# Reordering the first weight loads of a fused top-k attention and cosine feed-forward kernel

## The chip, the cores and the metric

The kernel runs on one core of a Trainium2 chip. The metric is device time in microseconds (us) of one execution. Four executions of the kernel before took 1467.93 to 1472.03 us, median 1469.47 us. In the text and in the profile, PE is TensorE (matmul), ACT is ScalarE, DVE is VectorE, POOL is GpSimd and SP is SyncE, which here only issues transfers (DMAs). "ACTq" and "SPq" are the queues from which those engines issue transfers.

## The reference

```python
def _attn_ref(q, k, v):                       # 8 batches, 8 heads, 576 positions, 64 wide
    scores = scale * np.matmul(q, k.transpose(0, 1, 3, 2))
    kth = np.partition(scores, -32, axis=-1)[..., -32:-31]
    scores = np.where(scores >= kth, scores, -1000000000.0)
    scores = scores - np.max(scores, axis=-1, keepdims=True)
    attn = np.exp(scores)
    attn = attn / (np.sum(attn, axis=-1, keepdims=True) + 1e-09)
    return np.matmul(attn, v).astype(np.float32)

def _moe_ref(x, w_in, w_out):                 # 4608 tokens, 512 -> 2048 -> 512
    h = x @ w_in
    g = h * np.cos(h)
    return (g @ w_out).astype(np.float32)
```

The attention output, with its heads laid side by side, is the x of the feed-forward block. The two weight matrices come as float64, all other inputs as float32.

## The kernel before, in words

A **unit** is 128 tokens by one pair of heads; there are 144 of them. One **slot** of the main loop (`slot`, line 720) handles each unit through a software pipeline. In slot i, DVE searches the 32 largest scores of unit i, with rows of 576 folded to 288 (`topk_first`, three `topk_round`s, and after the middle of the slot `topk_round(u, 3)` for the lesser halves, which reads `low`). POOL makes `low` for it (`fold_sum` L274, `fold_low` L283). ACT masks and exponentiates unit i-1 (L390, L392, L400) and takes the scores of unit i+1 out of PSUM (`take_scores`, L241 and L244). POOL splits the words of unit i-2 (`split`, L433 and L435), and SP writes them to DRAM and reads them back transposed (L443, L449). On even slots PE multiplies the transposed weights of two units by v (`values`, L486), and DVE writes the result to xT (L495). A slot starts on DVE with the fold L256.

Feed-forward work is fed into the slots as PE finds room (`feed`, `ff1` L546, `ff2` L621). Which piece goes where is fixed when the program is built, by a credit and by counts of what is ready; one of these counts is how many weight chunks were decoded by the slot before. An `ff2` piece also needs `g`, which POOL multiplies at L608.

**Weights.** They are float64 in DRAM and are decoded on the chip. There are 32 chunks of 128 rows by 512 numbers (512 KB each), 16 of w_in and 16 of w_out. `load_weights` (line 105) loads chunks into staging tiles `st`; the queue is ACT's unless another is given. `decode_first` does two ACT operations for each chunk (L136, L139), `decode_second` one DVE shift (L147), and `decode_third` one POOL addition (L157). In each slot the shifts stand in DVE's program after the third round of the search, so a shift that waits holds the rest of the search. The additions stand in POOL's program after `fold_low` of that slot and ahead of the `split` of the next. `decode_first` stands in ACT's program at the end of a slot.

**Order of loads before.** The prologue (from line 812) loads q and k of the first two pairs of heads and 2 chunks on SP's queue, then 6 chunks on ACT's queue, and then decodes 4 chunks. Slot 0 and slot 1 load q and k of pairs 2 and 3 and then v, on SP's queue; slot 1 loads 4 chunks, slots 2 and 3 load 3 chunks each, later slots 2 each, all on ACT's queue. The built program gives every transfer one of eight semaphores, and a transfer is issued only once the earlier transfer with the same semaphore has landed.

`BUSY` is a set of slots in which DVE makes `low` itself, with one more fold (L264), instead of POOL.

Of the kernel before, what the change touches and what calls it, by code (L numbers as in the profile page):

```python
# [30 lines left out]
def kernel(  # L31
# [9 lines left out]
    nc = tc.nc  # L41
# [6 lines left out]
    NP = H // 2  # L48
# [37 lines left out]
    for i in range(DF // CW):  # L86
        w = consts.tile([P, NC, CW], F32, tag=f"w_in{i}", name=f"w_in{i}")
# [4 lines left out]
    for f in range(NF):  # L92
        w = consts.tile([P, DM], F32, tag=f"w_out{f}", name=f"w_out{f}")
        w_out.append(w)
        chunks.append((moe_w_out[f * P : (f + 1) * P, :], w))
    CHUNKS, XB = 7, 4
    BUSY = range(7, 11)
    ff = {"live": 0, "tick": 0, "now": 0, "credit": 0.0, "end": False, "kind": 0, "half": 0, "open": 0}

    wq = {"next": 0, "loaded": deque(), "second": deque(), "third": deque(), "done": 0, "ready": 0}  # L100

    def staged(spare=0):
        return sum(c[2] == spare for k in ("loaded", "second", "third") for c in wq[k])

    def load_weights(n, queue=None):
        queue = queue or nc.scalar
        for _ in range(n):
            i = wq["next"]
            if i >= len(chunks):
                return  # L110
            src, dst = chunks[i]
            if not DECODE:
                queue.dma_start(out=dst, in_=src)
                wq["next"] = wq["done"] = i + 1
                continue
            spare = i < 3 * XB and i % 2 == 1 and staged(1) < XB
            if spare:
                st = ffw.tile([P, CW, 2], I32, tag="x", name="st", bufs=XB)
            elif staged() + ff["live"] >= CHUNKS:
                return  # L120
            else:
                st = ffw.tile([P, CW, 2], I32, tag="g", name="st", bufs=CHUNKS)
            queue.dma_start(out=st.rearrange("p w i -> p (w i)"), in_=src)
            wq["loaded"].append((st, dst, int(spare)))
            wq["next"] = i + 1
# [4 lines left out]
    def decode_first(n):  # L130


        for _ in range(min(n, len(wq["loaded"]))):
            st, w, spare = wq["loaded"].popleft()
            lo, hi = st[:, :, 0], st[:, :, 1]
            nc.scalar.activation(  # L136
                out=w, in_=hi.bitcast(F32), func=AF.Prelu, scale=2.0**-111, alpha=2.0**32
            )
            nc.scalar.mul(out=lo, in_=lo.bitcast(U32), mul=2.0**-29)  # L139
            wq["second"].append((st, w, spare))  # L140

    def decode_second(n):

        for _ in range(min(n, len(wq["second"]))):
            st, w, spare = wq["second"].popleft()
            wi = w.bitcast(I32)
            nc.vector.tensor_scalar(  # L147
                out=wi, in0=wi, scalar1=3, scalar2=None, op0=ALU.logical_shift_left
            )
            wq["third"].append((st, w, spare))  # L150

    def decode_third():

        while wq["third"]:
            st, w, _ = wq["third"].popleft()
            wi = w.bitcast(I32)
            nc.gpsimd.tensor_tensor(out=wi, in0=wi, in1=st[:, :, 0], op=ALU.add)  # L157
            wq["done"] += 1
# [91 lines left out]
    def fold_high(u):  # L250

        s, sc = u["s"], u["sc"]
        if u["n"] not in BUSY:
            del u["sc"]
# [5 lines left out]
    def fold_now(u):  # L260

        s, sc = u["s"], u.pop("sc")
        u["low"] = work.tile([P, 2, HS], F32, tag="low", name="low", bufs=1)
        nc.vector.tensor_tensor(  # L264
            out=u["low"], in0=sc[:, :, 0:HS], in1=s[:, :, HS:S], op=ALU.min
        )

    def fold_sum(u):

        if not u["folds"]:  # L270
            return
        s = u["s"].bitcast(I32)
        u["low"] = work.tile([P, 2, HS], F32, tag="low", name="low", bufs=1)
        nc.gpsimd.tensor_tensor(  # L274
            out=u["low"].bitcast(I32), in0=s[:, :, 0:HS], in1=s[:, :, HS:S], op=ALU.add
        )

    def fold_low(u):

        if not u["folds"] or u["n"] in BUSY:  # L280
            return
        low = u["low"].bitcast(I32)
        nc.gpsimd.tensor_tensor(  # L283
            out=low, in0=low, in1=u["rest"][:, :, HS:S].bitcast(I32), op=ALU.subtract
        )
# [15 lines left out]
    def topk_first(u, w):  # L301

        u["top"] = tops[u["n"] % len(tops)]
        merges = w and w["folds"]
        if merges:
            merge_first(w)
        if u["folds"]:
            if u["n"] not in BUSY:
                fold_sum(u)
            fold_high(u)  # L310
        else:
            u["rest"] = work.tile([P, 2, S], F32, tag="rest", name="rest", bufs=1)
        if merges:
            merge_second(w)
        if u["folds"] and u["n"] in BUSY:
            fold_now(u)
        topk_round(u, 0, [lambda: bounds(w), lambda: distances(w)] if w else ())

    def topk_round(u, rnd, between=(), ahead=None):
        top, rest, lasts = u["top"], u["rest"], TOPK // 8 - 1  # L320
        end = TOPK - 1 - 8 * rnd
        at = top[:, :, end : end - 8 if rnd < lasts else None : -1, 0]
        if u["folds"]:
            search(
                at, rest[:, :, HS:S] if rnd == 0 else rest[:, :, 0:HS], rest[:, :, 0:HS], rnd < lasts,
                between if rnd < lasts else (),
            )
        else:
            search(at, u["s"] if rnd == 0 else rest, rest, rnd < lasts, between)
        if rnd < lasts:  # L330
            return
        del u["rest"]
        if u["folds"]:
            low = u.pop("low")
            for k in range(TOPK // 16):
                more = k < TOPK // 16 - 1
                if ahead and not more:
                    take_values(ahead)
                search(
                    top[:, :, 1 + 8 * k : 9 + 8 * k, 1], low, low, more,  # L340
                    () if more or rnd < lasts else between,
                )
# [10 lines left out]
    def merge_second(u):  # L353
        nc.vector.tensor_reduce(
            out=u["top"][:, :, TOPK - 1, 1], in_=u.pop("lesser"), axis=mybir.AxisListType.X,
            op=ALU.max,
        )
# [57 lines left out]
    def both(u):  # L415
        return [lambda: sums(u), lambda: reciprocal(u)] if u else ()
# [151 lines left out]
    def take_banks():  # L568
        while full:
            take, *what = full.popleft()  # L570
            take(*what)
# [117 lines left out]
    at_slot, at_once = {}, {}  # L689
# [7 lines left out]
    for n in range(NP, len(order)):  # L697
        i = last[order[n - 5]] if n >= 5 else 0
        load_at(max(i, 2 * NP + 2), load_qk, *order[n])
        i = last_values[order[n - 6]] if n >= 6 else 0  # L700
# [2 lines left out]
    for hp in range(NP):  # L703
        at_once[hp] = [(load_v, 0, hp)]
    for hp in range(2, NP):
        at_once[hp - 2].insert(0, (load_qk, 0, hp))


    for i, u in enumerate(units):
# [4 lines left out]
    def send(x):  # L714

        split(x)
        write_halves(x)
        transposes(x)

    def slot(i, u, w, x, z):  # L720
        n = 0 if i == 0 else 4 if i == 1 else 3 if i < NP else 2
        if i < NP:
            for load, b, hp in at_once[i]:
                load(b, hp)
        load_weights(n)
        if x:
            send(x)
        topk_first(u, w)
        fold_low(u)
        topk_round(u, 1)  # L730
        topk_round(u, 2)
        decode_second(NP)
        decode_third()
        made = scored.get(i, [])
        if z:
            take_banks()
        feed(1)

        for m in made:
            scores(m)  # L740
        if z:
            values(z)


        late = len(made) > 0

        decoding = i < 3 * NP
        if i % 2 or decoding:
            sines(1)
        if w:  # L750
            mask(w)
        take_banks()
        if w and late:
            exponentials(w)
        take_scores(units[i + 1])
        if w and not late:
            exponentials(w)
        topk_round(u, 3, both(w), z)
        if i in at_slot:
            load, b, hp = at_slot[i]  # L760
            load(b, hp)
        gate(1)
        feed(1 if len(made) == 2 else 2)
        take_banks()
        decode_first(NP)
        reduce_first()
        reduce_second()
        feed(1 if len(made) == 2 else 3)
        if i == LAST:
            sines(1)  # L770
# [43 lines left out]
        nc.tensor.matmul(tt[:, 0:P], ones, ones, start=True, stop=True)  # L814
    load_qk(0, 0)
    load_qk(0, 1)
    load_weights(2, nc.sync)
    scores(units[0])
    take_scores(units[0])
    load_weights(2 * NP - 2)  # L820
    decode_first(NP)
    for i in range(NU + 1):
        ff["end"] = i >= NU
        ff["credit"] = min(ff["credit"] + 5.0 - 0.9 * len(scored.get(i, [])), 5.3)
# [2 lines left out]
        u, w = (units[i - n] if 0 <= i - n < NU else None for n in range(2))  # L827
# [53 lines left out]
```

## Time and profile before

| | |
|---|---|
| Median of four executions | 1469.47 us |
| Profiled execution, its own time | 1468.81 us |
| Its span in the profile | 1467.0 us |
| Mean granted TensorE clock | 0.971 |
| PE busy / DVE busy / ACT busy / POOL busy | 95% / 93% / 74% / 79% of the span |

Busy shares are means over stages that differ. The slots start on DVE (first instruction at L256) at these times in us from the start of the span: slot 0 at 7.82, 1 at 28.98, 2 at 39.31, 3 at 52.94, 4 at 62.93, 5 at 73.33, 6 at 82.99, 7 at 93.04, 8 at 103.33, 9 at 114.44. A timeline line reads: start, time from the first start to the last end of the merged instructions, engine, line, operation, output <- inputs, shapes, count, and in brackets how long the engine stood idle before and what released it.

### The profile page before, as it was taken

Reading aid. Unit: us, or ns where it says so; the run is one execution under the profiler, and the core shown is the slowest. Engines: PE = TensorE matmul, PEld = TensorE weight load, DVE = VectorE, ACT = ScalarE, POOL = GpSimd, SP = SyncE. Lnnn points to the kernel's source line nnn. Section 1 sums busy time; section 2 is a strip of 40 time slices with the busy share of each in tenths; the row PEclk is TensorE's granted clock in tenths of the full one; section 3 lists DMA queues with packets and bytes.
Section 4 is the critical chain, followed back from the end, with each engine's and each line's share of the span. In section 5 each row is a group of like instructions: output and inputs, shape, how many; then the busy total and the mean of one; then the engine's idle time right before and its main releaser. Section 6 shows DMA issues by size and latency. Waiting matters only on the chain.

```text
span 1467.0 us, 30264 instructions
## 1 busy us (share of the span) xinstructions
PE 1387.3 (95%) x10290; PEld 995.7 (68%) x10290; DVE 1363.2 (93%) x5213; ACT 1087.1 (74%) x1911; POOL 1163.4 (79%) x814
## 2 busy tenths in 40 slices
PE   4278899999999999999999999999999999999998
PEld 2155667777777767777777777777777776777765
DVE  5999999999999999999999999999999999999831
ACT  4677777777777777777777777777777787777651
POOL 3977888888888887888888888888888888888510
PEclk6579999999999999999999999999999999999999
DMA  8787576656665576656765666656665456655300
GB/s 264 221 238 209 164 200 158 160 156 183 189 162 149 148 200 170 163 151 177 197 170 148 146 176 190 176 143 175 192 169 159 144 166 175 168 151 143 71 8 15
DMA packets 427433, 239.99 MB, mean 164 GB/s; under 512 B 375952, under 2 KB 392592, under 8 KB 427280
## 3 DMA queue, kind: packets, MB, share of 16 engines
q1 hardware_dynamic: 417552, 212.69, 54.7%
q10 hardware_dynamic: 9728, 25.38, 5.1%
q8 instruction: 81, 1.33, 0.4%
q14 instruction: 72, 0.59, 0.1%
HBM read 45.09 MB, written 101.19 MB: 100 GB/s over the span
## 4 chain that ended last, share of the span: by engine, by line
PE 84%; DVE 10%; ACT 4%; DMA 1%; issue 0%; POOL 0%; SPq 0%; ACTq 0%; POOLq 0%
PE o L621 32%; PE mm L546 31%; PE rim L486 10%; PE sc L229 8%; DVE top L361 4%; DVE rest L366 2%; PE rim L229 2%; DMA st<-in_moe_w_in_dram 1%; DVE rest L256 1%; ACT s L400 1%; ACT s L392 1%; DVE low L366 1%; DVE w_in L147 1%; ACT L400 0%; ACT x L562 0%
## 5 line engine op out<-in xcount | busy, mean ns | idle before, releaser
L546 PEld LDWEIGHTS mm<-xT,w_in 128*128 128x128 f32 x4608 | 536.6, 192 | 71.9 <-issue 64.1
L621 PE MATMUL o<-w_out,g 128*128 128x512 f32 x1152 | 541.5, 604 | 8.9 <-POOL g L608 7.6
L546 PE MATMUL mm<-xT,w_in 128*128 128x128 f32 x4608 | 539.9, 275 | 5.2 <-DVE xT L495 3.2
L361 DVE MAX8 top<-rest 128x8 f32<-128x288 f32 x1148 | 480.9, 454 | 0.0
L433 POOL COPY halves<-s 128x2304 uint16<-128x2304 uint16 x140 | 294.7, 2105 | 149.7 <-ACT s L400 148.8
L366 DVE MATCH_REPLACE8 rest<-top,rest 128x288 f32<-128x288 f32 (+1 forms) x860 | 377.1, 446 | 0.0
L621 PEld LDWEIGHTS o<-w_out,g 128*128 128x128 f32 x1152 | 204.2, 192 | 199.7 <-issue 188.6
L361 DVE MAX8 top<-low 128x8 f32<-128x288 f32 x568 | 240.0, 448 | 0.0
L400 ACT ACTIVATE s<-s,nd 128x576 f32<-128x576 f32 x288 | 220.2, 767 | 1.2 <-ACT ob L631 0.4
L392 ACT ACTIVATE s<-s,top 128x576 f32<-128x576 f32 x288 | 206.1, 765 | 0.0
L283 POOL TENSOR_TENSOR low<-low,rest 128x576 int32<-128x576 int32 x138 | 195.0, 1413 | 10.8
L274 POOL TENSOR_TENSOR low<-s 128x576 int32<-128x576 int32 x138 | 195.0, 1413 | 7.4 <-ACT s L246 5.4
L229 PE MATMUL sc<-k,q 64*128 64x448 f32 (+1 forms) x640 | 154.9, 587 | 40.5 <-DVE rest L256 23.8
L560 ACT ACTIVATE g<-mm 128x512 f32<-128x512 f32 x144 | 85.8, 596 | 129.1 <-PE mm L546 125.1
L591 POOL TENSOR_TENSOR x<-g,x 128x1024 f32<-128x1024 f32 x68 | 160.9, 2367 | 5.7
L608 POOL TENSOR_TENSOR g<-g,x 128x1024 f32<-128x1024 f32 x68 | 160.9, 2366 | 1.9 <-ACT x L601 1.9
L486 PE MATMUL rim<-pT,v 128*64 128x128 f32 (+1 forms) x2560 | 158.5, 267 | 2.4 <-DMA pT<-rows 2.4
L486 PEld LDWEIGHTS rim<-pT,v 128*64 128x64 f32 x2560 | 131.9, 138 | 12.6 <-DMA pT<-rows 3.0
L241 ACT COPY s<-sc 128x896 f32<-128x896 f32 x143 | 128.2, 897 | 1.4 <-PE sc L229 1.4
L366 DVE MATCH_REPLACE8 low<-top,low 128x288 f32<-128x288 f32 x284 | 123.6, 443 | 0.0
L244 ACT COPY s<-rim 128x256 f32<-128x256 f32 x144 | 55.0, 382 | 90.5 <-PE rim L486 90.5
L229 PEld LDWEIGHTS sc<-k,q 64*128 64x128 f32 (+1 forms) x640 | 46.2, 181 | 102.8 <-DVE rest L366 46.4
(62 smaller groups left out, 1337.5 us busy)
## 6 DMA issues: line engine op xcount, KB each, us to landing
rows<-halves SPq DMA_DIRECT2D x140, 640.0 KB, 3.0
out_dram<-ob ACTq DMA_DIRECT2D x36, 256.0 KB, 2.2
q<-in_q_dram SPq DMA_DIRECT2D x31, 288.0 KB, 3.5
v<-in_v_dram SPq DMA_DIRECT2D x32, 256.0 KB, 3.2
st<-in_moe_w_out_dram ACTq DMA_DIRECT2D x16, 512.0 KB, 5.3
st<-in_moe_w_in_dram ACTq DMA_DIRECT2D x14, 512.0 KB, 5.8
k<-in_k_dram SPq DMA_DIRECT2D x31, 144.0 KB, 3.5
k<-in_k_dram SPq DMA_DIRECT2D x32, 128.0 KB, 3.7
```

Of the source, the lines that this page charges most:

```text
L229: nc.tensor.matmul(to[r0 : r0 + rows, j, 0 : k1 - k0], st["q"][d, q0 : q0 + rows], st["k"][d, k0:k1], start=True, stop=True,)
L274: nc.gpsimd.tensor_tensor(out=u["low"].bitcast(I32), in0=s[:, :, 0:HS], in1=s[:, :, HS:S], op=ALU.add)
L283: nc.gpsimd.tensor_tensor(out=low, in0=low, in1=u["rest"][:, :, HS:S].bitcast(I32), op=ALU.subtract)
L361: nc.vector.max(to[:, j], src[:, j])
L366: nc.vector.match_replace(rest[:, j], to[:, j], src[:, j], NEG)
L392: nc.scalar.activation(out=s[:, j], in_=s[:, j], func=AF.Prelu, bias=less[:, j, 1:2], scale=1.0, alpha=FAR)
L400: nc.scalar.activation(out=s[:, j], in_=s[:, j], func=AF.Exp, bias=nd[:, j : j + 1], scale=SCALE, accum_out=den[:, j, 0:1],)
L433: nc.gpsimd.tensor_copy(out=halves[:, :, 0 : 2 * S], in_=s.rearrange("p (k h) -> p h k", h=2))
L486: nc.tensor.matmul(o[d, to], lhsT, rhs, start=c == 0, stop=c == NT)
L546: nc.tensor.matmul(mm[:, at : at + w], w_in[f // FC][:, c, (f % FC) * P : (f % FC + 1) * P], blk["xT"][:, c], start=c == 0, stop=c == NC - 1,)
L591: nc.gpsimd.tensor_tensor(out=x, in0=g, in1=x, op=ALU.subtract)
L621: nc.tensor.matmul(o, g[:, at : at + P], w_out[f], start=f == 0, stop=f == NF - 1)
```

## The change

Five edits. The prologue loads 3 chunks on SP's queue and no chunk on ACT's, and decodes 3. Slots 0 and 1 load 3 and 4 chunks on SP's queue; from slot 2 on the chunks are on ACT's queue as before, and slot 2 loads 4 in place of 3. In slots 0 and 1, v of the slot's pair is now loaded ahead of q and k of the pair two on, and the chunks of the slot follow. `decode_third` takes the chunk shifted last first. `BUSY` also holds slot 11.

```diff
-    BUSY = range(7, 11)
+    BUSY = range(7, 12)
...
-    def load_weights(n, queue=None):
-        queue = queue or nc.scalar
+    def load_weights(n, queue):
...
         while wq["third"]:
-            st, w, _ = wq["third"].popleft()
+            st, w, _ = wq["third"].pop()
             wi = w.bitcast(I32)
...
     for hp in range(2, NP):
-        at_once[hp - 2].insert(0, (load_qk, 0, hp))
+        at_once[hp - 2].append((load_qk, 0, hp))
...
     def slot(i, u, w, x, z):
-        n = 0 if i == 0 else 4 if i == 1 else 3 if i < NP else 2
+        n = 4 if i in (1, 2) else 3 if i < NP else 2
...
-        load_weights(n)
+        load_weights(n, nc.sync if i < 2 else nc.scalar)
...
     load_qk(0, 0)
     load_qk(0, 1)
-    load_weights(2, nc.sync)
+    load_weights(3, nc.sync)
     scores(units[0])
     take_scores(units[0])
-    load_weights(2 * NP - 2)
-    decode_first(NP)
+    decode_first(3)
```

In the built program PE's order stays as it is, except that one `ff2` piece (two matmuls, four PE instructions) leaves the group between the scores of slot 8 and those of slot 10 and stands in slots 12 and 13 instead; the last chunk is decoded one slot later.

## The prediction

> **What bounds the kernel now.** I read the page first, then the busy time by stretches, then the timelines of the first 60 us. The page says that the chain that ended last is mostly PE.
>
> ```profile
> span 1467.0 us, 30264 instructions
> PE 1387.3 (95%) x10290; PEld 995.7 (68%) x10290; DVE 1363.2 (93%) x5213; ACT 1087.1 (74%) x1911; POOL 1163.4 (79%) x814
> PE 84%; DVE 10%; ACT 4%; DMA 1%; issue 0%; POOL 0%; SPq 0%; ACTq 0%; POOLq 0%
> ```
>
> That alone would say that an edit to loads is worth nothing. The stretches say where it isn't so (columns: PE, PE weight loads, DVE, ACT, POOL busy, granted clock, DMA share, GB/s; the second is the sum of a table over the first 60 us).
>
> ```profile
> 250.00:450.00 200.00, 200.00 (x1504) 145.67 (x1501) 197.72 (x771) 156.87 (x272) 172.13 (x118) 1.00 0.65 169
> sum 60.00, PE 19.68 PEld 10.73 DVE 42.71 ACT 33.51 POOL 35.38; mean PE 0.98 PEld 0.54 DVE 2.14 ACT 1.68 POOL 1.77
> ```
>
> From about 176 us to the tail PE never rests, and its order there stays the same. That part has a fixed length. What moves the end is only when PE gets there, and before some 90 us DVE decides: PE is busy 19.68 of the first 60 us. ACT's timeline, then DVE's, show what holds DVE:
>
> ```profile
> 7.14 0.64 ACT L246 COPY s<-sc 128x576 f32<-128x576 f32 x1
> 7.29 13.68 ACTq L123 DMA_DIRECT2D st<-in_moe_w_in_dram  x5
> 21.02 0.66 ACT L136 ACTIVATE w_in<-st 128x512 f32<-128x512 f32 x1 [13.23 <-DMA v_tail<-in_v_dram]
> ```
>
> ```profile
> 12.98 0.44 DVE L366 MATCH_REPLACE8 rest<-top,rest 128x288 f32<-128x288 f32 x1
> 21.71 0.43 DVE L147 TENSOR_SCALAR w_in<-w_in 128x512 int32<-128x512 int32 x1 [8.29 <-ACT w_in L136]
> 22.81 1.53 DVE L147 TENSOR_SCALAR w_in<-w_in 128x512 int32<-128x512 int32 x2 [0.67 <-ACT w_in L136]
> 25.05 0.74 DVE L147 TENSOR_SCALAR w_in<-w_in 128x512 int32<-128x512 int32 x1 [0.70 <-ACT w_in L136]
> 25.71 0.81 DVE L361 MAX8 top<-rest 128x8 f32<-128x288 f32 x2
> ...
> 34.63 1.42 DVE L147 TENSOR_SCALAR w_in<-w_in 128x512 int32<-128x512 int32 x4
> ...
> 44.96 4.72 DVE L147 TENSOR_SCALAR w_in<-w_in 128x512 int32<-128x512 int32 x4
> ```
>
> Chunk 0 landed at 10.36 us by the trace, yet ACT decodes it at 21.02: its queue stood in the six issues until 20.97. The sixth was issued at 20.63; its semaphore was that of the first v load, which landed at 20.61 (that v itself was issued at 11.96, when chunk 1 landed at 11.95). So the six issues held ACT, and ACT held the search of unit 0. The second loss is in slot 2: four shifts take 4.72 us, in slot 1 the same four 1.42. POOL's timeline at that time shows a fold and then the additions, each begun while shifts were still to come:
>
> ```profile
> 44.79 1.41 POOL L283 TENSOR_TENSOR low<-low,rest 128x576 int32<-128x576 int32 x1
> 46.62 5.44 POOL L157 TENSOR_TENSOR w_in<-w_in,st 128x512 int32<-128x512 int32 x4 [0.42 <-DVE w_in L147]
> ```
>
> **The change part by part.**
>
> *Loads.* One weight chunk alone takes 3.9 to 4.3 us from issue to landing (issues at 34.82 and 42.67); four in a row on ACT's queue alone, issued from 26.45, landed at 30.56, 31.86, 33.34 and 34.79, 1.41 apart. Between 7.33 (the second pair has landed) and 28.36 eight chunks, two pairs of q and k and three v landed; less 8 x 1.41 that leaves 9.7 us, so I estimate 1.9 for a pair and 2.0 for a v with its tails. In the new order on one queue: chunks 0 to 2 at 9.2 (issue 5.05 + 4.1), 10.6, 12.0; v 14.0; pair 2 at 15.9; chunks 3 to 5 at 17.3, 18.7, 20.1; v 22.1; pair 3 at 24.0; chunks 6 to 9 at 25.4, 26.8, 28.2, 29.7. SP issues all of this; a transfer waits for the landing of the one eight before it, which in this list is always more than 4 us ahead of need. Behind these on SP's queue stand only v of slot 2 and the write of unit 0's rows, which POOL gives at about 31.
>
> [...]
>
> *Slot 0.* Shifts come at 13.4 (end of the L366 row). Chunk 2's first ACT operation ends at 12.0 + 0.55, so no shift waits: three by 0.33 (1.42 for four, overlapping) end at 14.4. From 25.71 to the next slot's start, 28.98, are 3.27, so slot 1 starts at 17.7: **11.3 earlier**. The scores of unit 1 were done by PE at 8.6 and ACT copies them by 14.2.
>
> *Slots 1 to 4 by count.* A slot is 9.0 plus 0.33 a shift plus 0.40 for xT on even slots (slot 3: 9.99 with three shifts, slot 5: 9.66 with two). Slot 1 has three shifts for four (-0.33), slot 3 four for three (+0.33).
>
> *Deadlines on ACT*, which decodes in order ahead of mask, exponentials and copies (1.11 a chunk, then 1.5 + 1.7 + 1.1): chunk 5 done at 21.2, copies for slot 2 at 25.6, DVE wants them at 27.7: 2.1 spare. Chunk 9 done at 30.8, copies at 35.1, wanted at 38: 3 spare.
>
> *Reverse additions.* POOL now waits for the last shift, so no addition can fall between shifts. This takes away slot 2's stall: 4.72 - 1.42 = **-3.3**. The price: additions start (n-1) x 0.33 later (1.0 us for four), and the buffer of the chunk loaded first is freed last: chunk 16 waits for chunk 6's addition, at about 40, still 10 us ahead of its shift. POOL is the close second there: split 2.1 + 0.4, folds 2.9 and 1.27 an addition make 10.5 us in a slot of four, against 10.33 on DVE. Following POOL from 14.6: additions to 18.4, folds to 21.3, additions 24.5 to 28.3, split and folds to 33.6. Slot 2's shifts are due at 33.15: 0.5 late. Additions to 40.3, folds from 42.7 to 45.6; slot 3's shifts, due at 43.85, fall into them.
>
> The trace prices that: in slot 2 of before the first shift stood from 44.96 to 46.48 while L283 ran to 46.19. [...]
>
> *BUSY.* One fold on DVE in slot 11, +0.66, ahead of the bounds on which ACT and PE wait there: I count it whole; POOL's two folds saved (2.8) are worth nothing, as it rests 3 us in that slot. *The moved piece*, in PE's timeline:
>
> ```profile
> 126.34 5.33 PE L621 MATMUL o<-w_out,g 128*128 128x512 f32 x8 [2.36 <-POOL g L608]
> ```
>
> Half of this, 2.67 us, leaves the front of slot 10's scores, so DVE's wait of 1.39 at 136.61 goes: -1.4. Its 2.4 us reappear in slots 12 and 13, where PE idles 2.59 at 161.38. Bounds for both: -2 to +2.
>
> **Sum.** -11.3 - 0.33 - 3.3 + 0.33 + 4.0 + 0.66 - 1.4 = -11.3. The span becomes 1455.7, that execution 1457.5; its own time lay 0.66 under the median of the runs, so the forecast is 1469.47 - 11.3 = **1458.2 us**.
>
> **The rivals.** *No lock (20%).* [...] *ACT waits again (20%).* Chunks or rows land late; the DMA share is 0.95 to 1.07 from 8 to 22 us, and beyond the 2.1 spare each us at chunk 5 is a us of slot 2, while late rows hold `values` in slot 4. Five late cost 3 plus as much again there: about 1464. *Hidden (5%).* PE's 84% of the chain make the head worthless: 1469.5. Against it stands PE's 40 idle us of the first 60. *Slower (5%).* One queue does not pipeline a mix of large and small transfers: at 4 us a chunk and 2 to 3 for each smaller piece, chunk 5 comes after 45 instead of 20, and slot 2 some 15 later than now: 1480. It decides from chunk 5 landing after 33 (20.1 + 2.1 + 11). Against it: four chunks 1.41 apart on one queue.
>
> **How the numbers follow.** The forecast's case has 50%, with its own range 1456.3 to 1460.3. The range for 8 in 10 goes to the no-lock case below (1453.8) and to the late landings above (1463.5). A measurement of this kernel tells 0.2%, 2.9 us, from no change. Faster: 50 + 20 + 20 less a little for landings later still, 0.89; the same 0.06; slower 0.05.
>
> **What would show it.** Slot 1 starts on DVE at 17.7 (a start after 20 refutes the load order); no transfer issue on ACT before slot 2; slot 2's shifts near 2 us, those of slots 3 and 4 near 3 with L274 or L283 under them; slot 7 starts near 82 (93.04 now); no PE idle over 1 us after 176 less the gain. I am wrong if slot 7 gains and the end doesn't, or if ACT's first decode in slot 1 waits past 22.

## The result and the profile after

The changed kernel takes 1466.23 us by the median of 43 runs (1462.65 to 1472.01), the kernel before 1469.36 by the median of 64. The ratio is 0.9976, with a 95% interval of 0.9968 to 0.9983: 3.1 us by the medians, 3.5 by the ratio. The forecast was 11.3 us. The sign was right, the size not, and 1466.23 lies above the range (1453.8 to 1463.5). The profiled execution took 1465.85 us, its span is 2.96 shorter than before. Here are the page's head and the chain's shares:

```profile
span 1464.1 us, 30242 instructions
...
PE 1387.6 (95%) x10290; PEld 999.4 (68%) x10290; DVE 1361.9 (93%) x5214; ACT 1088.4 (74%) x1911; POOL 1157.7 (79%) x812
...
PE 82%; DVE 9%; ACT 5%; DMA 2%; POOL 1%; issue 1%; SPq 0%; ACTq 0%; POOLq 0%
```

DMA holds 2% of the chain where it held 1%: the write and the transposed read of unit 1's rows, which weren't on it before, are now. The stretches (PE, PE weight loads, DVE, ACT, POOL busy, granted clock, DMA share, GB/s; then the sum over the first 60 us) show a middle as full as before and a head with more DVE work in it, 51.46 us where it was 42.71:

```profile
250.00:450.00 200.00, 200.00 (x1440) 144.94 (x1441) 197.50 (x771) 156.57 (x276) 171.57 (x118) 1.00 0.63 168
...
sum 60.00, PE 22.88 PEld 14.59 DVE 51.46 ACT 40.05 POOL 42.06; mean PE 3.81 PEld 2.43 DVE 8.58 ACT 6.67 POOL 7.01
```

ACT's timeline, then DVE's (start, time, engine, line, operation; in brackets the idle time before and its releaser; past line 105 the changed file's line numbers are one less):

```profile
9.88 0.67 ACT L135 ACTIVATE w_in<-st 128x512 f32<-128x512 f32 x1 [2.22 <-DMA st<-in_moe_w_in_dram]
```

```profile
13.22 1.09 DVE L146 TENSOR_SCALAR w_in<-w_in 128x512 int32<-128x512 int32 x3
...
33.15 1.54 DVE L146 TENSOR_SCALAR w_in<-w_in 128x512 int32<-128x512 int32 x4
...
44.86 1.52 DVE L146 TENSOR_SCALAR w_in<-w_in 128x512 int32<-128x512 int32 x4
...
55.29 2.85 DVE L146 TENSOR_SCALAR w_in<-w_in 128x512 int32<-128x512 int32 x2
58.06 0.41 DVE L146 TENSOR_SCALAR w_out<-w_out 128x512 int32<-128x512 int32 x1
```

Chunk 0 is decoded when it lands, at 9.88 instead of 21.02, and the first shifts, at 13.22, wait for nothing. Slot 2's four shifts (33.15) take 1.54 where they took 4.72. Here is the table of slots, from one start of the search on DVE to the next; the lead is by how much a slot starts earlier than in the kernel before.

| slot | before | after | moved | forecast |
|---|---|---|---|---|
| 0 | 21.17 | 9.82 | -11.35 | -11.3 |
| 1 | 10.33 | 9.99 | -0.34 | -0.33 |
| 2 | 13.63 | 11.70 | -1.93 | -3.3 |
| 3 | 9.99 | 10.44 | +0.45 | +0.33 |
| 4 | 10.39 | 14.75 | +4.36 | 0 |
| 2 to 4 together | 34.01 | 36.89 | +2.88 | +1.03 (-3.3 + 0.33 + 4.0) |
| 10, 11 | 12.17, 9.66 | 10.69, 10.29 | -1.48, +0.63 | -1.4, +0.66 |
| 14, 15 | 9.38, 9.09 | 12.22, 9.87 | +2.84, +0.78 | 0 |
| the last slot and what follows | 104.04 | 106.05 | +2.0 | 0 |

The lead is 13.29 us at slot 4, more than the whole forecast, and 8.93 at slot 5. It is 9.47 at slot 14, 5.86 at slot 16, 4.97 in the last slot and 2.96 at the end. So the head was won as foretold, and three places took most of it back: slot 4 (4.36), slots 14 and 15 (3.62) and what follows the last slot's start (2.0). The chain of slot 4 shows the first (start, length, what):

```profile
44.74 7.66 DMA rows<-halves
52.41 7.54 DMA pT<-rows
59.95 0.14 issue
60.09 2.42 PE rim L485 x20
62.53 0.38 ACT s L243
62.94 0.49 DVE xT L494 x2
```

SP's timeline shows when the rows of unit 1 were issued, and behind what, first in the kernel before, then in the changed one:

```profile
48.63 2.84 SPq L449 DMA_TRANSPOSE pT<-rows  x1
...
54.47 0.37 SPq L443 DMA_DIRECT2D rows<-halves  x1
```

```profile
35.62 7.20 SPq L448 DMA_TRANSPOSE pT<-rows  x1
...
44.74 0.62 SPq L442 DMA_DIRECT2D rows<-halves  x1
52.41 5.29 SPq L448 DMA_TRANSPOSE pT<-rows  x1
```

POOL has unit 1's rows ready at 42.24, 3.03 after slot 3's start (1.50 before). SP stands in the transposed read of unit 0 until 42.82 and then issues v. The write goes out at 44.74, 5.53 after slot 3's start; before it was 54.47, 1.53 after it. The round trip takes 15.21 us and took 14.79 before (54.47 to 69.26): nearly the same. So the rows land 10.30 into slot 4, where it was 6.33.

### The profile page after: what moved, and what is told of

Same layout as the page of the kernel before. It is cut to its first block, busy times and chain, and to the rows that moved or that the text cites. A ratio compares the mean times of both kernels' runs of the same rounds, so it can differ in the third digit from the quotient of the medians.

```text
span 1464.1 us, 30242 instructions
## 1 busy us (share of the span) xinstructions
PE 1387.6 (95%) x10290; PEld 999.4 (68%) x10290; DVE 1361.9 (93%) x5214; ACT 1088.4 (74%) x1911; POOL 1157.7 (79%) x812
## 4 chain that ended last, share of the span: by engine, by line
PE 82%; DVE 9%; ACT 5%; DMA 2%; POOL 1%; issue 1%; SPq 0%; ACTq 0%; POOLq 0%
PE mm L545 31%; PE o L620 31%; PE rim L485 10%; PE sc L228 7%; DVE top L360 4%; DVE rest L365 2%; PE rim L228 2%; ACT s L399 1%; ACT s L391 1%; DVE rest L255 1%; ACT L399 1%; DMA k<-in_k_dram 1%; DMA rows<-halves 1%; DMA pT<-rows 1%; DVE low L365 1%
## 5 line engine op out<-in xcount | busy, mean ns | idle before, releaser
L545 PEld LDWEIGHTS mm<-xT,w_in 128*128 128x128 f32 x4608 | 539.4, 193 | 78.4 <-issue 64.3
L545 PE MATMUL mm<-xT,w_in 128*128 128x128 f32 x4608 | 543.0, 276 | 11.0 <-DVE xT L494 7.1
L559 ACT ACTIVATE g<-mm 128x512 f32<-128x512 f32 x144 | 85.8, 596 | 129.4 <-PE mm L545 125.3
L485 PE MATMUL rim<-pT,v 128*64 128x128 f32 (+1 forms) x2560 | 159.5, 269 | 6.1 <-DMA pT<-rows 6.1
L485 PEld LDWEIGHTS rim<-pT,v 128*64 128x64 f32 x2560 | 132.8, 139 | 16.2 <-issue 7.4
L255 DVE TENSOR_TENSOR rest<-sc,s 128x576 f32<-128x576 f32 x142 | 106.2, 748 | 6.8 <-ACT s L245 6.6
```

Source lines behind the costliest of these rows:

```text
L485: nc.tensor.matmul(o[d, to], lhsT, rhs, start=c == 0, stop=c == NT)
L545: nc.tensor.matmul(mm[:, at : at + w], w_in[f // FC][:, c, (f % FC) * P : (f % FC + 1) * P], blk["xT"][:, c], start=c == 0, stop=c == NC - 1,)
```

## The experiments

Each ratio is to the kernel before, whose median was 1469.58 beside the first four kernels, 1469.95 beside the next three and 1470.01 beside the last two. A slot's length, a lead and a timeline are those of one profiled execution. The theory: slot 4 loses to the rows' round trip, made long by the weight chunks beside it, and slot 14 to the moved `ff2` piece. The rivals: shifts locked by POOL's folds cost slot 4 (by a lock is meant here only that shifts beside POOL's folds or additions take longer, as in slot 2 of the kernel before: 4.72 us for four, 1.42 in slot 1); less traffic there only moves the traffic; and, for the last two kernels, it is the late issue of the rows and not the traffic.

**The moved piece**, `e_ff2` (one more chunk in slot 4, so that PE's order is that of the kernel before):

```diff
-        n = 4 if i in (1, 2) else 3 if i < NP else 2
+        n = 4 if i in (1, 2) else 3 if i <= NP else 2
```

> The changed kernel with one more chunk in slot 4 (3 in place of 2), so that the 32nd chunk is decoded as early as before and PE's order is that of the kernel before to the last instruction. Theory: slots 14 and 15 of the changed kernel are 3.6 us longer than before because the moved ff2 piece puts take_first behind it on PE and ACT, and POOL's reduce, split and fold_low queue behind that. Then slots 14 and 15 take 18.5 us together (22.1 changed, 18.5 before), the lead at slot 16 is 9 to 9.5 us, and the time is 3 to 4 us under the changed kernel, 1462 to 1463. Rival: the stall comes from the phase in which POOL and ACT stand after the shorter head, whatever PE's order; then slot 14 stays near 12 us and the time near 1466.

Measured: 1463.81 us (10 runs), ratio 0.9961 (0.9946 to 0.9975), span 1462.0. Slots 14 and 15 take 9.38 and 9.09, as before, and the lead is 9.04 at slot 16 where it was 5.86. The median is 2.4 us under the changed kernel's, less than the 3 to 4 expected, and the intervals (0.9968 to 0.9983 there) still overlap; it is the slots that show the cause. In the changed kernel POOL and then DVE show why the piece costs there:

```profile
159.64 1.05 POOL L581 TENSOR_SCALAR x<-x 128x1024 f32<-128x1024 int32 x1 [2.92 <-ACT x L561]
160.77 2.39 POOL L590 TENSOR_TENSOR x<-g,x 128x1024 f32<-128x1024 f32 x1
...
166.99 1.40 POOL L282 TENSOR_TENSOR low<-low,rest 128x576 int32<-128x576 int32 x1
```

```profile
168.42 0.82 DVE L360 MAX8 top<-low 128x8 f32<-128x288 f32 x2 [2.73 <-POOL low L282]
```

With two matmuls of `ff2` in the way, the `ff1` group ahead of `take_first` (L559, L561) ends so late that ACT does it behind its exponentials, at 158.41. POOL, in order, stands 2.92 us, does two reductions, then the split, and only then makes `low`; DVE's search of slot 14 waits 2.73 for it.

This kernel also tells of the lock in slot 4. Its shifts there are not held:

```profile
55.03 0.75 DVE L146 TENSOR_SCALAR w_in<-w_in 128x512 int32<-128x512 int32 x2
55.70 0.42 DVE L146 TENSOR_SCALAR w_out<-w_out 128x512 int32<-128x512 int32 x1
```

yet its slot 4 takes 15.04, no less than the 14.75 of the changed kernel, whose shifts lost 2.1 us (55.29 to 58.47, against 1.09 for three). The transposed rows landed at 59.98 in the one and at 59.95 in the other. The lock was there in the changed kernel, hidden behind the rows.

**Fewer chunks in slots 2 and 3, more from slot 4 on**, `e_light`:

```diff
-        n = 4 if i in (1, 2) else 3 if i < NP else 2
+        n = 4 if i == 1 else 2 if i in (2, 3) else 3 if i < 8 else 2
```

> The changed kernel with 2 chunks in each of slots 2 and 3 and 3 in slots 4 to 7 (PE's order as before the change). Theory: slot 4 is 4.4 us too long because weight transfers on the other queue hold the write and the transposed read of unit 0's and unit 1's rows (issue of the first read 7.2 us, second landing at 59.95). Then the first transposed read issues in under 4 us, unit 1's read lands before 55, xT in slot 4 waits for nothing, slot 4 takes 10.1 to 11, the lead at slot 7 is 12 to 14 us, and the time is 1457 to 1460. Rival: the shifts that fall under POOL's folds make slot 4 long; with 2 shifts in it they lose about as much, 1.5 to 2, slot 4 takes 12 or more and the lead at slot 7 is at most 11. Second rival: the traffic only moves to slots 4 to 7, whose rows then come late: slot 6 or 8 longer than 12.

Measured: 1468.39 us (22 runs), ratio 0.9986 (0.9973 to 0.9999). Slot 4 falls to 12.34, and slots 6, 8, 9 and 10 rise to 12.58, 12.26, 13.42 and 12.73: the lead is 12.00 at slot 5 and 5.13 at slot 11. The round trip still took 14.67 us (42.28 to 56.95), in a stretch with a DMA share of 0.97. The expected 1457 to 1460 was far off: DVE waits at xT for 2.19 in slot 4, and then for 1.97 in slot 6 and 1.01 in slot 8 (none and 0.29 in the changed kernel). Thinning one slot moves the wait and adds to it.

**The load order alone**, `e_loads` (the additions in their old order, `BUSY` to slot 10):

```diff
-    BUSY = range(7, 12)
+    BUSY = range(7, 11)
...
-            st, w, _ = wq["third"].pop()
+            st, w, _ = wq["third"].popleft()
```

> The changed kernel with additions in the order of shifts and slot 11 not in BUSY, so the load order alone. Theory (rows decide slot 4): the lock between additions and shifts costs 2 to 3 us in slots 2 or 3, but the rows of unit 1 are late anyway, so the lead at slot 5 is 8 to 9 us as in the changed kernel, and the time is within 1 us of it. Rival (the reversal is worth its 3 us): lead at slot 5 only 6, time 1469.

Measured: 1464.94 us (7 runs), ratio 0.9958 (0.9942 to 0.9973), against 0.9976 (0.9968 to 0.9983) with all five edits; the intervals just overlap. Slot 2 takes 11.65 and its four shifts 1.42, slot 3 takes 10.34, slot 4 14.84, and slots 14 and 15 are as long as in the changed kernel. The reversed additions bring nothing in the changed kernel: with the new order of loads slot 2 has no stall for them to take away.

**The reversed additions alone, on the kernel before**, `e_pop`:

```diff
-            st, w, _ = wq["third"].popleft()
+            st, w, _ = wq["third"].pop()
```

> The kernel before with the reversed additions alone. Theory: slot 2, 13.6 us before, becomes 11.4 to 11.6 (the fold still locks the first shift, 1.1), slots 0 and 4 as before; lead at slot 7 about 2 us, time 1467. Rival: a later start of POOL's additions is given back at slots 3 to 5: lead at slot 7 under 0.5, time 1469.

Measured: 1471.8 us (22 runs), ratio 1.0015 (1.0002 to 1.0028). Slot 2 falls by 2.62 (11.01), slot 3 rises by 1.49 (11.48), and the lead is 1.36 at slot 7 and 0.68 at slot 12; slot 18 gives back 1.44, with DVE's wait at xT at 3.43 where it was 1.99. By the last slot the lead is -2.6, so the small loss of the median is there in the profile; why slot 18 and later ones lose was not tested. DVE's and POOL's timelines of this kernel show the lock both ways:

```profile
44.58 1.42 DVE L147 TENSOR_SCALAR w_in<-w_in 128x512 int32<-128x512 int32 x4
55.59 2.57 DVE L147 TENSOR_SCALAR w_in<-w_in 128x512 int32<-128x512 int32 x3
```

```profile
44.70 2.58 POOL L283 TENSOR_TENSOR low<-low,rest 128x576 int32<-128x576 int32 x1
```

At 44.58 the shifts were first: they ran their 1.42 and the fold of 1.41 took 2.58. At 55.59 a fold (L274, 54.58 to 56.00) was first and the next fold came between the shifts, and three shifts of 1.09 took 2.57. Each side lengthened the other here, the fold by 1.17 in slot 2 and the three shifts by 1.48 in slot 3, which is what slot 3 lost (1.49); by what means is not shown.

**No weight traffic behind the first 13 chunks**, `e_noload`. This is the kernel with the piece put back, and it leaves out the loads of chunks 13 to 31: their decoding reads, at the same sizes, a small tile of 128 columns of chunk 13 over and over, so that their weights are not those of the reference. All other work is the same.

```diff
-            queue.dma_start(out=st.rearrange("p w i -> p (w i)"), in_=src)
+            if i == 13:
+                wq["from"] = consts.tile([P, P, 2], I32, tag="from", name="from")
+                queue.dma_start(out=wq["from"].rearrange("p w i -> p (w i)"), in_=src[:, 0 : 2 * P])
+            if i < 13:
+                queue.dma_start(out=st.rearrange("p w i -> p (w i)"), in_=src)
...
+            if wq["index"].popleft() >= 13:
+                lo_in, hi = (wq["from"][:, :, k].unsqueeze(1).to_broadcast([P, 4, P]) for k in range(2))
...
```

> The changed kernel with one more chunk in slot 4 (the kernel of e_ff2), and with the loads of chunks 13 to 31 left out: their decoding stays, instruction for instruction, but reads a small tile of chunk 13 that is loaded once. So 19 transfers of 512 KB are gone from slots 2 to 10 and nothing else. Theory (the transposing of rows shares the DMA engines with the weights and ends slot 4): the first transposed read issues in under 4 us (7 with the loads), unit 1's lands before 53 (60 with them), DVE has no wait at xT in slot 4, slot 4 takes 10.4 to 12.4 (15.0 with the loads; what is over 10.4 is the lock between folds and shifts), the lead at slot 7 is 11.5 to 13.5 us (8.4 with them), the time 1458 to 1461. Rival (the lock, or POOL as such, makes slot 4): slot 4 over 13.5 and the lead at slot 7 under 10.

Measured: 1458.98 us (6 runs), ratio 0.9922 (0.9904 to 0.9941), against 0.9961 with the loads. Slot 4 takes 11.05, and the lead at slot 7 is 11.65; the forecast's sum makes 10.6 there (its 11.3 is for the end). SP's timeline:

```profile
43.83 0.54 SPq L451 DMA_DIRECT2D rows<-halves  x1
47.55 2.80 SPq L457 DMA_TRANSPOSE pT<-rows  x1
```

The write goes out nearly as late as with the piece put back and the chunks loaded (4.16 us after slot 3's start, 4.36 there), but lands in 3.71 instead of 7.62 and the read in 4.84 instead of 9.10: a round trip of 8.56 where it was 16.73 (15.21 in the changed kernel). The DMA share over this round trip is 0.70, against 1.02 over that of the changed kernel. So the traffic is a cause: with nearly the same late issue but without the chunks, DVE's wait at xT in slot 4, 3.90 us with them, is gone. Most of what slot 4 has over 10.39 is a wait of 0.56 for `low`.

**v later**, `e_latev2` and `e_latev3`. The next two are the kernel with the piece put back, and load v of pair i in slot i + 2 (whose loads now run to slot 5). The second also loads three chunks in slot 2 and three in slot 5 (the last two lines of the cut below are its own).

```diff
-        at_once[hp] = [(load_v, 0, hp)]
+        at_once[hp + 2] = [(load_v, 0, hp)]
...
-        at_once[hp - 2].append((load_qk, 0, hp))
+        at_once[hp - 2] = [(load_qk, 0, hp)]
...
-        n = 4 if i in (1, 2) else 3 if i <= NP else 2
+        n = 4 if i == 1 else 3 if i < NP + 2 else 2
```

> The kernel of e_ff2 with the four early loads of v moved two slots later (v of pair i loaded in slot i + 2, still before use in slots 4 and 6). Theory: the v loads are 2 us each and stand ahead of chunks 3 to 9, so chunk 9 lands near 29.5 in place of 33.2, ACT's late exponentials no longer hold slot 2 (10.3 to 10.6 in place of 11.7), unit 0's rows get through sooner, slot 4 loses 1 to 3 us in place of 4.4, and the lead at slot 7 is 10 to 12 us; time 1460 to 1462. Rival: the DMA engines are short over the whole head, so what is moved out of slots 0 and 1 comes back in slots 4 to 6: lead at slot 7 still 8 to 9, time 1464.

Measured: 1461.6 us (6 runs, 1459.79 to 1463.54), ratio 0.9942 (0.9922 to 0.9963). Without the six v transfers in the list, chunk 9 lands at 28.05 instead of 31.96 and slot 2 takes 10.45 instead of 11.67. Slot 4 is back at 10.39, but slot 3 takes 14.92. ACT's timeline:

```profile
47.57 0.33 ACTq L122 DMA_DIRECT2D st<-in_moe_w_out_dram  x1
47.95 0.20 ACT L389 ACTIVATE nd<-nd 128x2 f32<-128x2 f32 x1 [8.34 <-DVE low L365]
```

The profile names DVE as the releaser, but what the mask needs of DVE (L382) was done at 39.60. ACT's queue had stood since 39.20 at the issue of a chunk: one of its waits ended at 47.21, after v had landed at 47.17, and the issue went out at 47.57, after v's last tail (47.52) and the first of POOL's additions (47.44), which frees a buffer; which of these two came last the trace doesn't tell. DVE then waited 3.83 us for the exponentials. It is the hold that the change took out of slot 0, back in slot 3.

> As e_latev2, with 4 chunks in slot 1 and 3 in each of slots 2 to 5 in place of 4, 4, 3, 3 in slots 1 to 4: one chunk less ahead of unit 0's and 1's rows, one more after them. Theory: slot 4 a us or so shorter than in e_latev2, slot 6 no longer, lead at slot 7 11 to 13 us, time 1459 to 1461. Rival (short DMA engines over the whole head): slot 6 or 8 longer by what slot 4 wins, the same lead at slot 11.

Measured: 1462.32 us (13 runs, 1457.88 to 1470.81), ratio 0.9941 (0.9924 to 0.9959). Its profiled execution, at 1457.88, is the lowest of its runs: slots 2 to 4 take 10.46, 10.68 and 12.47, and the lead at slot 7 is 10.97. By the median it is no better than the one above it.

**The rows ahead of v**, `e_vlast` and `e_latev4`. If the late issue matters too, putting v of pairs 2 and 3 behind the rows should help (first on the kernel with the piece put back, then on the last one, whose v of pairs 0 and 1 are both loaded in slot 2):

```diff
...
         if x:
             send(x)
+            if 3 <= i <= NP:
+                load_v(0, i - 1)
```

> This kernel is the changed one with three chunks in slot 4 (so that PE's order is that of the kernel before), and with v of pairs 2 and 3 loaded behind the rows of slots 3 and 4 on SP's queue, where they stood in front of them. It asks whether it is the late issue of rows(1) that costs slot 4. Theory (late issue times slow round trip): v's three issues, 41.40 to 43.2 us, no longer stand between the transposed read of unit 0 and the write of unit 1's rows, so that the write goes out at about 41.9, 1.3 earlier, and 272 KB less lie in front of it: pT of unit 1 lands at 57 or earlier instead of 59.98, slot 4 takes 12 to 13.1 instead of 15.04, the start of slot 5 is 11 us ahead of the kernel before, and the time is 1461.5 to 1462.5 against 1463.8. Rival (the weight chunks alone set the round trip, whatever the issue): pT lands at 59 to 60, slot 4 stays at 14 to 15, the time at 1463 to 1464.

Measured: 1462.2 us (6 runs), ratio 0.9944 (0.9927 to 0.996), which overlaps the 0.9961 (0.9946 to 0.9975) without the edit. Slot 4 takes 15.78, not 12 to 13.1, and the answer is mixed. The write went out 3.67 after slot 3's start (4.36 without the edit); it no longer waited for SP, which was free at 43.00, but for POOL, whose rows were ready at 43.61. The round trip took as long as ever, 16.48 us (16.73). The rows landed at 9.09 in slot 4 instead of 10.61, of which 0.56 is only that slot 3 was longer. What they would have won was lost on ACT:

```profile
60.19 0.97 ACTq L122 DMA_DIRECT2D st<-in_moe_w_out_dram  x2
61.20 0.20 ACT L389 ACTIVATE nd<-nd 128x2 f32<-128x2 f32 x1 [7.53 <-DMA v<-in_v_dram]
```

Two issues of chunks went out only after the transposed rows (60.11) and the moved v (60.75) had landed, and the mask behind them waited 7.53 us. v was put where ACT's issue waits for it. The profiled execution also lost 1.15 in slot 1 and 0.56 in slot 3.

> Late v with three chunks in slots 2 to 5, as in the run before it of that kind, but v of pairs 0 and 1 both in slot 2 and v of pairs 2 and 3 behind the rows of slots 3 and 4. Theory: the write of unit 1's rows goes out at about 42.7 instead of 44.63, its transposed rows land by 55.5 instead of 57.18, and xT's wait of 0.79 in slot 4 is gone: slot 4 takes 11.7 instead of 12.47, what is left above 10.4 being shifts that stand behind a fold. Slots 0 to 3 stay at 10.5, 10.0, 10.5 and 10.7. The start of slot 5 is 12.5 us ahead of the kernel before, and the time is 1 us under the run without this edit, 1461 by the median. Rival (loads of v that come later hold ACT's issues through shared semaphores): ACT's masks of slot 4 or 5 wait, DVE waits for den more than 2 us there, and the time is 1464 or more.

Measured: 1461.98 us (8 runs, 1458.05 to 1467.91), ratio 0.9939 (0.9918 to 0.996). Slot 4 takes 11.20, a little better than expected, and the lead is 13.57 at slot 5. Then slot 6 takes 17.23. POOL had unit 3's rows ready at 62.42, but SP stood in the transposed read of unit 2 until 64.81 and then issued the moved v; the write went out at 68.39 and landed at 75.73. POOL's next copy waited for it:

```profile
75.85 2.59 POOL L432 COPY halves<-s 128x2304 uint16<-128x2304 uint16 x1 [5.45 <-DMA rows<-halves]
```

Behind it DVE waited 4.43 for `low`, and then 2.21 at xT, for unit 3's rows, which landed at 82.60. Neither theory had named that place; the expected gain of 1 us over the run above is not there.

The rows of unit 1, in the profiled executions, tell how late issue and traffic share slot 4:

| kernel | write issued after slot 3's start | round trip | lands in slot 4 at | slot 4 |
|---|---|---|---|---|
| before | 1.53 | 14.79 | 6.33 | 10.39 |
| changed | 5.53 | 15.21 | 10.30 | 14.75 |
| load order alone | 5.43 | 15.32 | 10.40 | 14.84 |
| piece put back | 4.36 | 16.73 | 10.61 | 15.04 |
| fewer chunks in slots 2 and 3 | 4.15 | 14.67 | 7.96 | 12.34 |
| late v, three chunks in slot 2 | 6.22 | 12.55 | 8.09 | 12.47 |
| no chunks after the 13th | 4.16 | 8.56 | 2.37 | 11.05 |
| reversed additions alone | 4.72 | 13.05 | 6.29 | 10.54 |
| late v, four chunks in slot 2 | 8.04 | 10.17 | 3.29 | 10.39 |
| rows ahead of v | 3.67 | 16.48 | 9.09 | 15.78 |
| late v and rows ahead of it | 4.71 | 13.53 | 7.56 | 11.20 |

From the second row to the sixth, slot 4 is the landing plus 4.4, so 6.0 would be the deadline for a slot of 10.4. Part of the 4.4 is PE's clock. After its wait PE does the twenty instructions of `values` in 2.42 us at a granted clock of 0.50 (60.09 in the chain above); in the kernel before they took 1.31 at 1.00:

```profile
69.31 1.09 PE L486 MATMUL rim<-pT,v 128*64 128x128 f32 x16 [0.95 <-DMA pT<-rows]
70.23 0.39 PE L486 MATMUL rim<-pT,v_tail 128*64 128x128 f32 x4
```

That is why the landing at 6.33 cost nothing there; at the full clock the deadline is about 7 (an estimate: 6.0 and the 1.1 between the two). In the row "rows ahead of v" it is the mask, not the rows, that ends the wait, and slot 3 is longer in the two rows above it (11.48 and 14.92), so that rows issued late in it are in time for slot 4. In the last row DVE had no wait at xT. Against the kernel before, the lateness of 4.0 in the changed one is the issue's; the chunks' traffic is why the round trip takes 15 us, in both, and not 8.6.

The five kernels with the late v, the rows ahead or the piece put back have medians between 1461.6 and 1463.81, below both given kernels. No two of them can be told apart by their intervals; those of the four with v moved (up to 0.9963) end below that of the changed kernel (from 0.9968), that of the piece put back alone (up to 0.9975) does not.

## Why the prediction was wrong, point by point

*Where it was right.* The hold of ACT in six issues was the cause of slot 0's length, and its price was right: 11.35 for 11.3. So were slot 1 (-0.34 for -0.33) and `BUSY` (+0.63 for +0.66). Slot 0 was close: chunk 2 landed at 13.15, 1.1 later than the sum had it, and in `e_loads` the third shift did wait for it, 0.70. Still, slot 1 starts at 17.2 to 18.0 in all nine kernels with this prologue. Of the signs it named, slot 1 starts at 17.51 (17.7), and ACT issues no chunk before 33.19, in slot 2; slot 7 starts at 84.11, 2 later than named (near 82). The rival "hidden" fell too: of the 5.86 us of lead at slot 16, 4.97 reach the last slot. But that part was not of fixed length, as the prediction had it: slot 90 gives back 0.79, where a weight load of PE waits 0.94 for k (at 882.03), as none did before, and with the piece put back slots 54 and 90 give back 1.7 together. What decides how much was not tested.

*Right in number, not in cause: slot 10.* It won 1.48, and -1.4 was the forecast, for half of a piece that leaves PE's front. PE's timeline of the changed kernel, then of the one with the piece put back:

```profile
117.80 1.98 PE L620 MATMUL o<-w_out,g 128*128 128x512 f32 x4 [1.10 <-POOL g L607]
```

```profile
118.29 3.70 PE L620 MATMUL o<-w_out,g 128*128 128x512 f32 x8 [2.68 <-POOL g L607]
```

With all eight instructions back, slot 10 still takes 10.69. They take 3.70 us at a granted clock of 1.00, where the kernel before took 5.33 at 0.69 (from 126.34 to 131.74), and DVE's wait at xT, 1.39 before, is gone either way. The kernel without the chunks' loads shows the reverse: the same eight take 5.40 there (granted clock 0.65 from 114 to 118 us, 0.90 from 118 to 121), xT waits 1.60, slot 10 takes 12.38. So the 1.48 came from where PE's clock happened to stand, and that it met the forecast is luck.

*Slot 4, the step that failed first.* The sum gave slot 4 nothing but a part of the +4.0. That "late rows hold `values` in slot 4" stood among the rivals at 20%, and its own figure, 1464, lay outside the range that was to hold it. What the step missed is SP. It counted "only v of slot 2 and the write of unit 0's rows" behind the loads on SP's queue and gave deadlines to ACT alone. The rows of unit 1 come 1.5 later from POOL, then stand behind a transposed read that holds SP for 7.20 us (2.84 before) and behind v, and start 4.0 later in their slot. With a round trip of 15.2 they land 4.0 later in slot 4, PE then does its part at half the clock, and slot 4 lost 4.36. Without the chunks' traffic nearly the same late issue left no wait at xT.

*The moved piece, the second.* Its bounds of -2 to +2 covered slots 10 to 13. What mattered was one slot on: PE's group, ACT's `take_first`, POOL's reductions and `low`, DVE's search. That cost 3.62 in slots 14 and 15, and with the piece put back both slots are at their old length.

*Slot 2, a term mis-sized.* It won 1.93 and not 3.3. The estimate put chunk 9 at 29.7 with 3 us to spare; it landed at 33.16, and DVE waited 1.07 for ACT (0.80 for den, 0.27 at the next fold). A v with its tails was taken as 2.0 us. In the six kernels with this list of loads chunk 9 landed at 31.96 to 33.95, in the three with two v taken out of it at 27.24 to 28.05: by the means (33.1 and 27.6) each v cost 2.7. That is 1.4 of the 3.5 that chunk 9 was late; the rest is spread over the list. Chunk 0 alone took 4.88 and not 4.1, a time read in part from a chunk (34.82) that was not alone: two more were issued by 35.67. The DMA shares (second last number) of the changed kernel, then of the one with late v, say what a v does to the queue:

```profile
14.00:17.00 3.00, 0.78 (x2) 0.55 (x3) 3.00 (x11) 1.48 (x3) 2.50 (x3) 0.50 0.82 236
17.00:20.00 3.00, 2.23 (x8) 1.11 (x6) 2.97 (x12) 1.24 (x2) 2.92 (x4) 0.50 0.87 305
```

```profile
14.00:17.00 3.00, 1.82 (x5) 1.35 (x7) 3.00 (x11) 1.50 (x4) 2.63 (x3) 0.50 1.03 348
17.00:20.00 3.00, 1.10 (x6) 0.47 (x3) 2.97 (x13) 2.50 (x5) 2.92 (x3) 0.50 1.05 329
```

In the changed kernel the v tails of 16 KB in this list take 6.9 to 8.3 us from issue to landing, the chunks of 512 KB 4.6 to 8.7: a tail holds one of the eight semaphores about as long as a chunk, and fewer large transfers are under way. That this is the way in which v lowers the share is inferred; that the share rises without v is measured. It also answers the rival "one queue does not pipeline": one queue moved 348 and 329 GB/s, much as the two queues of the kernel before (313 and 380 in the same stretches). And the -3.3 was put down to the wrong edit: with the load order alone, the additions in their old order, slot 2's four shifts take 1.42. They came at 33.36, just after POOL's fold had ended (33.34), so the stall was gone before the reversal could take it away; on the kernel before, the reversal did take 2.62 off slot 2.

*Slot 3 and the +4.0.* The 4.0 that the sum adds over slots 2 to 4 for shifts beside POOL's folds was the author's estimate, and no run shows it. In the changed kernel the shifts of slots 2, 3 and 4 take 1.54, 1.52 and 3.18 us; undisturbed, four take 1.42 and three 1.09, so 2.3 came in place of the 4.0. In slot 3 the shifts, due by the prediction at 43.85, came at 44.86, since DVE had waited 1.07 in slot 2, and by then the fold had 0.24 left. One delay took the place of the other. The 2.1 in slot 4 did come, but lay beside the wait for the rows.

*The tail.* It was taken as fixed, and is 2.0 us longer. Windows over 17 us from the start of the last slot, the kernel before first:

```profile
1363.00:1380.00 17.00, 15.08 (x133) 11.89 (x132) 15.06 (x51) 12.99 (x23) 8.99 (x7) 1.00 0.42 113
```

```profile
1358.00:1375.00 17.00, 15.08 (x103) 11.78 (x103) 15.08 (x51) 11.38 (x22) 9.02 (x7) 0.90 0.39 107
```

PE rests 1.92 us in both. Then, in the changed kernel, the granted clock is 0.50 from 1368.8 to 1372.2, and two groups of PE (L545, L485) take 4.57 us where they took 2.97: 1.6 of the 2.0. Before, the clock stays at 1.00. Of the eleven kernels profiled, three (this one, the one with the piece put back and the one with fewer chunks) have a tail of 106.0 to 106.2, the others of 104.0 to 104.5. Over 1358 to 1375 us the mean granted clock is 0.90 in this one and in the one with the piece put back, and 1.00 in seven others, the one with fewer chunks among them; where that one loses its 2 us is not shown. What decides where the clock falls wasn't tested.

## What to carry to other kernels

When a change lets the search start earlier, give every round trip behind it a deadline: when its write can be issued on its queue, behind what, and how long it takes beside the traffic of that time (here 15.2 us against 8.6 without). Follow every piece of work that is moved through all engines that it feeds, one stage further than where it lands. A wait taken out by moving loads can come back wherever the loads go; it did in four of the kernels here.

## What the runs showed of the hardware that was not expected

The issue of a transposed read holds SP's queue for 2.38 to 4.88 us in the kernel before and 2.37 to 7.20 in the changed one, and for 7.49 once with the rows ahead of v (35.51). It took 2.80 with no weight chunk in flight (47.55 without the chunks), where the same read took 5.69 with the piece put back and the chunks loaded, and 7.20 with four in flight (35.62 in the changed kernel). The number of chunks is not all: beside two it took 3.26 in the kernel before (61.09) and 5.29 in the changed one (52.41). The same 640 KB write of unit 1's rows landed in 3.71 us with no chunk in flight and in 7.62 beside them, in the same two kernels. The time from issue to landing of one transposed read ranged from 4.5 to 10.3 us in the kernel before and from 4.5 to 9.3 in the changed one.

Where the half clock falls moves a kernel of this length by 1.6 us in each of two places: one piece of eight PE instructions at slot 10 (3.70 or 5.33), and the two groups in the tail (2.97 or 4.57), where the half clock lasted from 1368.8 to 1372.2, 3.4 us. The same rest of PE, 1.92 us, stands ahead of the two groups in both given kernels: in the one before the granted clock stayed at 1.00 behind it, in the changed one it fell to 0.50. What decides between the two no run here shows.
